# Block 3's state projection by Strassen's scheme between two output pairs, with seeded accumulators, in a fused state-space and gated layer

## Chip, cores and metric

One core of a Trainium2 chip runs the whole program. The metric is the device time of one execution in microseconds (us), and lower is better. The engines are TensorE (PE, matmuls), VectorE (DVE), ScalarE (ACT), GpSimd (POOL) and the DMA queues.

## The reference

```python
xn = layernorm(A_x)                                  # 2048 x 512, bf16
# A: diagonal complex state space, P = 512 states
Bu = einsum("bld,pd->blp", xn, B_bar)                # the state projection
h_t = Lam_bar * h_{t-1} + Bu_t                       # over 2048 steps
yA = 2 * real(einsum("blp,dp->bld", h, Cmat)) + xn * Dskip
# B: gated feed-forward, F = 1792
yB = (silu(xn @ w1) * (xn @ w3)) @ w2
out = A_x + yA + yB
```

The kernel works on four blocks of 512 rows. Each block needs its gates (14 tiles of 128 features), its state projection (4 state tiles, real and imaginary), a scan, and two output products of 256 rows each. These eight products are called "pairs" 0 to 7; pairs 0 and 1 belong to block 0, pairs 2 and 3 to block 1, and so on.

## The kernel before: what the argument touches

The output products already use Strassen's scheme in Winograd's form: seven block products in place of eight, with sums of blocks made by DVE (S1 to S4 of the left factor, called row sums here, and others of the right one). So does the up side (`w3`) of 12 of the last block's 14 gate tiles (the up scheme). The state projection is plain:

```python
def bu(b):                                  # state projection of block b
    for hf in range(NPT // 2):
        u = up.tile([P, 2, 2, TBLK], BF16, name="u")
        ...
                    for dt in range(NDT):   # 32 matmuls of 512 columns in all
                        nc.tensor.matmul(out=ps, lhsT=bt[:, ri, dt, ...], rhs=xnT_blk[b][:, dt, :], ...)
                    nc.scalar.activation(out=u[:, j, ri, :], in_=ps, func=ACT.Copy)
```

One output pair is seven products of 11 matmuls each (256 columns), seven for the gates and then four for the states. A seed is a value that is put into an accumulator in PSUM before the matmuls add to it. These are a pair's seeds, its fourth and its seventh product:

```python
def seeds(n):
    ...                                     # PSUM tiles g, e, f, z
    for t, cols in halves:                  # ACT puts the residual into e
        nc.scalar.activation(out=t, in_=o2[:, DH + cols.start:DH + cols.stop], func=ACT.Copy)

def product4():
    mms(z, v["a22"], tsum[3], True)
    ...
def product7():
    mms(g, v["s3"], tsum[2], False)
    add(q[2], g, o2[:, D1])                 # three adds on DVE
    add(o2[:, D2], g, q[1])
    add(o2[:, D1], z, q[2])
    store(c1 + 1, o2)
```

DVE's queue is put in order while the program is built. A small model, `Filler`, counts the microseconds given to PE (`bg.tensor`) and to DVE (`bg.own`, and a cost for each background task), and it lets background work in when DVE is not too far ahead:

```python
def own(self, us, after=0.1):
    self.dve = max(self.dve, self.pe + after) + us
def fill(self, lead=None):
    limit = self.pe + (self.lead if lead is None else lead)
    while self.tasks and self.dve + 0.5 * self.tasks[0][0] <= limit:
        ...
        self.pop()
```

The end of the program, in order, before the change:

```python
bu(3)
posts = ssm_tasks(3, True, between=up_sums(3))
...
y_fast(2, ...); y_fast(3, ...)
gate = glu_last(3)                          # the last block's gates ("gate stretch")
gate()
for n in range(4, 8): y_fast(n, ...)
```

## Time and profile before

The median is 203.09 us in three runs (202.9 to 203.15). The first table of the profile's page gives each engine's busy time, its share of the span and its instructions (PEld is the loading of weights, which overlaps PE):

```profile
span 201.1 us, 3551 instructions
## 1 busy us (share of the span) xinstructions
PE 197.2 (98%) x1353; PEld 126.4 (63%) x1353; DVE 180.4 (90%) x256; ACT 127.2 (63%) x257; POOL 47.9 (24%) x70
```

A busy PE can still contain gaps, because the recorded matmuls overlap: those of 512 columns are recorded as 379 ns long and start 216 ns apart. Start times are the better reading: from 8.2 us to the last matmul at 197.95 us, one matmul starts 216 ns (512 columns), 109 ns (256) or 56 ns (128) after the last. After the start there is one gap over 0.03 us. In the timeline of PE (start, duration, instruction, count, and in brackets the idle time before it and what ended it) it is the second line, where 0.67 us separate two starts of which 0.33 us are three matmuls of 256 columns:

```profile
85.80 0.49 PE L865 MATMUL gu_ps<-tw 128*128 128x256 f16 x3
86.47 0.82 PE L539 MATMUL gu_ps<-xnT,w_sb 128*128 128x512 bf16 x3 [0.18 <-DMA xnT<-xn]
```

The gap is 0.34 us long: block 2's gates wait for its transposed input, and only the 0.18 us in which the modelled matmuls don't cover it is listed as a wait.

The table of windows sums each engine's busy time in stretches that I cut at the first matmul of each stage. They are pairs 0 and 1; state projection of block 3 with pairs 2 and 3; gate stretch; pairs 4 to 7:

```profile
core 0: us, PE busy (x) PEld busy (x) DVE busy (x) ACT busy (x) POOL busy (x), PEclk, DMA share, GB/s
69.32:86.47 17.15, 16.97 (x155) 14.98 (x154) 16.56 (x25) 13.29 (x34) 4.66 (x7) 1.00 0.58 109
117.56:141.28 23.72, 23.72 (x188) 18.21 (x186) 21.78 (x30) 7.45 (x15) 6.56 (x5) 1.00 0.68 99
141.28:164.33 23.05, 23.05 (x151) 14.47 (x148) 22.09 (x32) 17.86 (x33) 0.86 (x1) 1.00 0.40 66
164.33:197.95 33.62, 33.62 (x330) 30.39 (x329) 26.36 (x44) 5.12 (x15) 2.84 (x2) 1.00 0.31 53
```

PE is the bound in all of them, with DVE close behind (21.78 of 23.72, 22.09 of 23.05). The tail, from the timeline of all engines (lines of PE left out), has three DVE adds of the seventh product, then two of the third:

```profile
196.98 0.42 DVE L876 TENSOR_TENSOR q<-y_ps,xn 128x256 f32<-128x256 f32 x1 [2.00 <-PE y_ps L865]
...
197.65 0.41 DVE L876 TENSOR_TENSOR xn<-y_ps,q 128x256 bf16<-128x256 f32 x1
...
198.09 0.81 SPq L882 DMA_DIRECT2D out_dram<-xn  x2
198.21 0.29 DVE L876 TENSOR_TENSOR xn<-gu_ps,x_blk 128x128 bf16<-128x128 f32 x1
198.53 0.37 ACTq L882 DMA_DIRECT2D out_dram<-xn  x1
```

### The profile page before, as it was taken

The numbers are of one execution on the slowest core, as the hardware profiler recorded it, in microseconds if no ns is written. First come the engines' busy times: TensorE is split into PE (matmuls) and PEld (weight loads), VectorE is DVE, ScalarE is ACT, GpSimd is POOL, SyncE is SP. The second block draws the span as 40 slices with busy tenths as digits, with TensorE's granted clock in tenths as the row PEclk, the third lists the DMA queues.
The fourth block names the chain that finished last, engine by engine and source line by source line (L and its number), as shares of the span: only waits on it lengthen the run. The fifth ranks groups of instructions, "written<-read, shape, count | busy, mean of one in ns | idle before, by whom it ended". The sixth has DMA issues, their size and how long they took to land.

```text
span 201.1 us, 3551 instructions
## 1 busy us (share of the span) xinstructions
PE 197.2 (98%) x1353; PEld 126.4 (63%) x1353; DVE 180.4 (90%) x256; ACT 127.2 (63%) x257; POOL 47.9 (24%) x70
## 2 busy tenths in 40 slices
PE   8999999999999999999999999999999999999994
PEld 2974444444444588844444445888566678888893
DVE  4699699999999999989999989998989998988833
ACT  4799788699999967957797676110588771101110
POOL 7160289600310053043005011315100003100000
PEclk9999999999999999999999999999999999999999
DMA  5999995980582043925895955294960002951011
GB/s 160 328 248 258 290 157 170 347 216 0 105 156 55 0 91 68 177 87 106 132 157 104 97 106 108 17 156 80 163 148 0 3 0 15 113 104 52 10 62 39
DMA packets 34225, 23.56 MB, mean 117 GB/s; under 512 B 21792, under 2 KB 32160, under 8 KB 34208
## 3 DMA queue, kind: packets, MB, share of 16 engines
q0 software_dynamic: 8096, 9.84, 32.3%
q1 hardware_dynamic: 25536, 13.21, 26.6%
q10 hardware_dynamic: 576, 0.30, 0.5%
q8 instruction: 10, 0.16, 0.3%
q14 instruction: 7, 0.06, 0.1%
HBM read 7.74 MB, written 2.10 MB: 49 GB/s over the span
## 4 chain that ended last, share of the span: by engine, by line
PE 59%; DVE 33%; DMA 3%; issue 2%; POOL 1%; ACT 1%; DVEq 0%
PE gu_ps L865 13%; PE gu_ps L539 12%; PE y_ps L865 7%; PE gu_ps L671 7%; PE bu_ps L865 4%; DVE u L484 4%; DVE act L557 4%; PE y_ps L438 3%; PE bu_ps L438 3%; PE y_ps L693 3%; DMA xnT<-xn 3%; DVE tw L796 2%; PE bu_ps L194 2%; DVE u L467 2%; DVE p L463 2%
## 5 line engine op out<-in xcount | busy, mean ns | idle before, releaser
L539 PE MATMUL gu_ps<-xnT,w_sb 128*128 128x512 bf16 x312 | 68.2, 379 | 0.2 <-DMA xnT<-xn 0.2
L539 PEld LDWEIGHTS <-w_sb 128*128 128x128 bf16 x312 | 30.4, 98 | 36.8 <-DMA xnT<-xn 0.5
L865 PEld LDWEIGHTS <-act 128*128 128x128 f16 x462 | 43.5, 98 | 5.4
L549 ACT ACTIVATE u<-gu_ps 128x512 bf16<-128x512 f32 x41 | 24.8, 606 | 5.8 <-PE gu_ps L539 5.1
L548 ACT ACTIVATE g<-gu_ps 128x512 bf16<-128x512 f32 x41 | 24.7, 603 | 5.4 <-PE gu_ps L539 5.1
L438 PEld LDWEIGHTS <-bt 128*128 128x128 bf16 x128 | 12.5, 98 | 15.1
L484 DVE TENSOR_TENSOR_SCAN u<-rho,act,u 128x512 bf16<-128x512 f32 x16 | 19.8, 1269 | 0.0
L824 POOL DMA_DIRECT2D act<-act x4 | 8.0, 2002 | 33.8 <-DVE tw L820 28.9
L865 PE MATMUL gu_ps<-w_sb,act 128*128 128x256 bf16 (+3 forms) x126 | 15.9, 267 | 0.0
L671 PE MATMUL gu_ps<-xnT,w_sb 128*128 128x512 bf16 x64 | 15.9, 379 | 0.0
L438 PE MATMUL y_ps<-xnT,bt 128*128 128x512 bf16 x64 | 15.1, 379 | 0.0
L438 PE MATMUL bu_ps<-xnT,bt 128*128 128x512 bf16 x64 | 15.1, 379 | 0.0
L557 DVE TENSOR_TENSOR act<-g,u 128x1024 f16<-128x1024 bf16 x21 | 14.2, 678 | 0.6 <-ACT u L549 0.6
L501 POOL DMA_DIRECT2D act<-p x7 | 6.3, 907 | 32.2 <-DVE act L494 28.2
L683 ACT ACTIVATE g<-gu_ps 128x512 bf16<-128x512 f32 x14 | 8.4, 598 | 5.7 <-PE gu_ps L671 5.3
L440 ACT ACTIVATE u<-y_ps 128x512 bf16<-128x512 f32 x16 | 9.5, 595 | 2.3 <-PE y_ps L438 2.1
L440 ACT ACTIVATE u<-bu_ps 128x512 bf16<-128x512 f32 x16 | 9.5, 595 | 2.0 <-PE bu_ps L438 1.9
L865 PE MATMUL bu_ps<-w_sb,act 128*128 128x256 bf16 (+3 forms) x84 | 10.4, 264 | 0.0
L865 PE MATMUL gu_ps<-ct,act 128*128 128x256 f16 (+1 forms) x72 | 10.4, 267 | 0.0
L484 DVE TENSOR_TENSOR_SCAN u<-rho,ends,u 128x512 bf16<-128x512 f32 x8 | 10.0, 1271 | 0.0
L467 DVE TENSOR_TENSOR u<-u,tabe 128x2048 bf16<-128x2048 bf16 x8 | 9.8, 1220 | 0.1
L490 DVE TENSOR_TENSOR p<-u,tabe 128x2048 f16<-128x2048 bf16 x8 | 9.8, 1220 | 0.1
(163 smaller groups left out, 342.3 us busy)
## 6 DMA issues: line engine op xcount, KB each, us to landing
act<-p POOLq DMA_DIRECT2D x7, 512.0 KB, 5.2
xn<-x_blk POOLq DMA_DIRECT2D x4, 512.0 KB, 5.8
out_dram<-xn SPq DMA_DIRECT2D x15, 128.0 KB, 2.6
w_sb<-in_B_w_dram SPq DMA_DIRECT2D x1, 1792.0 KB, 8.0
w_sb<-in_B_w_dram SPq DMA_DIRECT2D x2, 768.0 KB, 5.9
u<-x_blk POOLq DMA_DIRECT2D x3, 512.0 KB, 6.5
act<-act POOLq DMA_DIRECT2D x4, 352.0 KB, 6.8
w_sb<-in_B_w_dram SPq DMA_DIRECT2D x4, 256.0 KB, 4.3
```

Source lines behind the costliest of these rows:

```text
L438: nc.tensor.matmul(out=ps, lhsT=bt[:, ri, dt, pt * P:(pt + 1) * P], rhs=xnT_blk[b][:, dt, :], start=(dt == 0), stop=(dt == NDT - 1))
L440: nc.scalar.activation(out=u[:, j, ri, :], in_=ps, func=ACT.Copy)
L467: nc.vector.tensor_tensor(out=st["g"], in0=st["g"], in1=tabe[:, psl, 0:1, :].to_broadcast(FULL), op=ALU.mult)
L484: nc.vector.tensor_tensor_scan(out=v, data0=rho[:, pt:pt + 1].to_broadcast([P, TBLK]), data1=v, initial=init, op0=ALU.mult, op1=ALU.add)
L490: nc.vector.tensor_tensor(out=st["p16"][:, :, ::-1, :], in0=st["g"], in1=tabe[:, psl, 1:3, :], op=ALU.mult)
L539: nc.tensor.matmul(out=ps[:, tsl], lhsT=w[:, dt, f * P:(f + 1) * P], rhs=xnT[:, dt, tsl], start=(dt == 0), stop=(dt == NDT - 1))
L548: nc.scalar.activation(out=g16[:, f % 2, :], in_=g_ps, func=ACT.Silu)
L549: nc.scalar.activation(out=u16[:, f % 2, :], in_=u_ps, func=ACT.Copy)
L557: nc.vector.tensor_tensor(out=act(b)[:, k0:k1 + 1:k1 - k0, :], in0=g16, in1=u16, op=ALU.mult)
L671: nc.tensor.matmul(out=ps, lhsT=w[:, dt, f * P:(f + 1) * P], rhs=xnT[:, dt, :], start=(dt == 0), stop=(dt == NDT - 1))
L683: nc.scalar.activation(out=g16[:, f % 2, :], in_=side(w1_sb, f), func=ACT.Silu)
L865: nc.tensor.matmul(out=out, lhsT=left[:, k, :], rhs=right[k][:, cols], start=(start and k == 0), stop=(k == NK - 1), skip_group_check=True)
```

## The change

The intent is fewer columns on PE. The state projection of the last block is done by seven products in place of eight, one after another between the products of pairs 2 and 3. The sums of weights that this needs are written over the weights, which nobody needs afterwards. To make room on DVE, ACT seeds the accumulator Z (one DVE add less in each pair), S4 of pair 5 is an accumulating DMA, the up scheme covers 8 gate tiles rather than 12, and block 3's scans come later.

```diff
-    NG = 3
+    NG = 2
+    LATER = (4, 5)
+    def bu_fast(b, hf):            # returns five steps of seven products
+        def product(out, left, right, start=False):
+            for h in range(2):
+                for k in range(2):
+                    nc.tensor.matmul(out=out[:, h * TH:(h + 1) * TH], lhsT=left[:, h, k, :], rhs=right[:, k, :], ...)
+        def five():
+            product(e, s13, t1, True)
+            copy(s5, e)
+            subtract(s13, a22, s2)
 ...
+        return deque(((one, five), (two, six), (seven,), (three,), (four,)))
 ... in seeds():
+        nc.scalar.activation(out=z, in_=o2[:, D1], func=ACT.Copy)
 ... in y_fast():
-            mms(z, v["a22"], tsum[3], True)
+            mms(z, v["a22"], tsum[3], False)
+            copy(q[2], z)
-            add(q[2], g, o2[:, D1])
+            add(o2[:, D1], g, q[2])
             add(o2[:, D2], g, q[1])
-            add(o2[:, D1], z, q[2])
+            if n == 5:
+                gp.dma_start(out=v["s4"], in_=v["s2"], accum_op=ALU.add)
+            if i == 3 and n in LATER:
+                later[n] = product3        # done after product 5 of the next pair
 ... at the end:
-    bu(3)
-    posts = ssm_tasks(3, True, between=up_sums(3))
+    ssm_tasks(3, middle=[(0.0, after_y2, None), *row_sums(4, *pairs[4])])
-    y_fast(2, row_sums(3, *pairs[3]))
+    y_fast(2, row_sums(3, *pairs[3]), bu_fast(3, 0))
-    y_fast(3, row_sums(4, *pairs[4]))
+    y_fast(3, (), bu_fast(3, 1))
```

Left out are the sums' helpers, the homes of buffers, signs of some differences that were turned so that a DMA can add, and where in the program some tasks (seeds, gate multiplications, single row sums) are put in.

More of the change, by code (lines that the diff above doesn't have):

```diff
@@ L294, in ln_scalar_engine @@
             for cl in range(CPB):
-                spread.append((("ln", b, fn is norm and cl == CPB - 1), lambda fn=fn, cl=cl: fn(cl)))
+                spread.append(((fn.__name__, b, cl), lambda fn=fn, cl=cl: fn(cl)))
     NP3 = 3 * NPT
@@ L458, in pre_a @@
                 st["g"] = u_blk[b, hf]
-                if b == NBLK - 1 or (b, hf) == (2, 1):
-                    st["p"] = x_blk[2 if b == 2 else 2 + hf].rearrange("p (j r) t -> p j r t", r=2)
+                if (b, hf) in ((2, 1), (3, 0)):
+                    st["p"] = x_blk[b].rearrange("p (j r) t -> p j r t", r=2)
+                elif b == NBLK - 1:
+                    st["p"] = xtp.tile([P, NDT, TBLK], BF16, name="xnT").rearrange("p (j r) t -> p j r t", r=2)
                 else:
@@ L478, in scan @@
                 init = 0.0
-                if b == 1:
+                if b in (1, 2):
                     init = ends[:, hf, 2 * j + ri:2 * j + ri + 1]
-                elif b > 1:
+                elif b > 2:
                     init = act_blk[b - 1][:, k_state(pt, ri), TBLK - 1:TBLK]
@@ L501, in post_c @@
                     gp.dma_start(out=act_state(b, hf), in_=st["p16"], accum_op=ALU.add)
+            if (b, hf) == (1, 1):
+                pre_c.ready = lambda: ("squares", 2, CPB - 1) in sins_done
             pre_a.ready = lambda: (b, hf) in u_blk
@@ L640, with column_sums, run, column_list @@
     ups = {}
+    def column_sums(b):
+        def run():
+            for fn in column_list(b) + bu_first_sums():
+                fn()
+        run.ready = lambda: ("norm", b, CPB - 1) in sins_done
+        return [(2.1, run, "cols")]
+    def column_list(b):
+        xnT = xnT_blk[b]
+        t = x_blk[2].bitcast(FP16).rearrange("p a (k t) -> p a k t", k=2)
+        t1, t2, t3, t4 = (t[:, i] for i in range(4))
+        b11, b12, b21, b22 = (xnT[:, 2 * i:2 * i + 2, j * TH:(j + 1) * TH] for i in range(2) for j in range(2))
+        ups.update(t=(t1, t2, t3, t4), b=(b11, b12, b21, b22))
+        return [lambda out=out, x=x, z=z: nc.vector.tensor_tensor(out=out, in0=x, in1=z, op=ALU.subtract)
+                for out, x, z in ((t1, b12, b11), (t2, b22, t1), (t3, b22, b12), (t4, b21, t2))]
@@ new lines, in bu_quarter, with bu_first_sums, copy, parts @@
+    def bu_quarter(hf, kh, r, half=False):
+        v = bt[:, :, 2 * kh:2 * kh + 2, (2 * hf + r) * P:(2 * hf + r + 1) * P]
+        return v.bitcast(FP16) if half else v
+    def bu_first_sums():
+        return [lambda hf=hf: nc.vector.tensor_tensor(
+            out=bu_quarter(hf, 0, 1, True), in0=bu_quarter(hf, 0, 1), in1=bu_quarter(hf, 1, 1), op=ALU.add)
+            for hf in range(2)]
+    def bu_fast(b, hf):
+        t1, t2, t3, t4 = ups["t"]
+        b11, b12, b21, b22 = ups["b"]
+        a11, a12, a22 = bu_quarter(hf, 0, 0), bu_quarter(hf, 1, 0), bu_quarter(hf, 1, 1)
+        s2, s4, s13 = (bu_quarter(hf, *i, True) for i in ((0, 0), (1, 0), (0, 1)))
+        u = up.tile([P, 2, 2, TBLK], BF16, name="u")
+        s5 = glup.tile([P, 2, TBLK], BF16, name="g16").bitcast(FP32).rearrange("p a t -> p (a t)")
+        if hf == 0:
+            f, z = (ps_bu.tile([P, TBLK], FP32, name="bu_ps") for _ in range(2))
+            e, g = (ps_y.tile([P, TBLK], FP32, name="y_ps") for _ in range(2))
+        else:
+            f, z, e, g = (ps_gu.tile([P, TBLK], FP32, name="gu_ps") for _ in range(4))
+        def product(out, left, right, start=False):
+            for h in range(2):
+                for k in range(2):
+                    nc.tensor.matmul(out=out[:, h * TH:(h + 1) * TH], lhsT=left[:, h, k, :], rhs=right[:, k, :],
+                                     start=(start and h == 0 and k == 0), stop=(k == 1), skip_group_check=True)
+            bg.tensor(0.436)
+        def copy(out, x):
+            nc.scalar.activation(out=out, in_=x, func=ACT.Copy)
+        def parts(ps):
+            return ps.rearrange("p (h t) -> p h t", h=2)
+        def subtract(out, x, y):
+            bg.own(0.4)
+            nc.vector.tensor_tensor(out=out, in0=x, in1=y, op=ALU.subtract)
+        def add(out, ps):
+            bg.own(0.7)
+            nc.vector.tensor_tensor(out=out, in0=parts(ps), in1=parts(s5), op=ALU.add)
+        def one():
+            product(g, a11, b11, True)
+            copy(f, g)
+            subtract(s2, s13, a11)
+        def five():
+            product(e, s13, t1, True)
+            copy(s5, e)
+            subtract(s13, a22, s2)
+        def two():
+            product(f, a12, b21)
+            subtract(s4, a12, s2)
+            copy(u[:, 0, :, 0:TH], parts(f))
+        def six():
+            product(g, s2, t2)
+            copy(e, g)
+        def seven():
+            product(g, s13, t3)
+            copy(z, g)
+            add(u[:, 1, :, TH:TBLK], g)
+        def three():
+            product(e, s4, b22)
+            add(u[:, 0, :, TH:TBLK], e)
+        def four():
+            product(z, a22, t4)
+            copy(u[:, 1, :, 0:TH], parts(z))
+            u_blk[b, hf] = u
+        return deque(((one, five), (two, six), (seven,), (three,), (four,)))
@@ L642, in up_sums @@
     def up_sums(b):
-        xnT = xnT_blk[b]
         n = 4 * NG * P
@@ L649, in up_sums @@
         s3 = up_quarter(0, 1, True)
-        t = xtp.tile([P, NDT, TBLK], BF16, name="xnT").bitcast(FP16).rearrange("p a (k t) -> p a k t", k=2)
-        t1, t2, t3, t4 = (t[:, i] for i in range(4))
-        b11, b12, b21, b22 = (xnT[:, 2 * i:2 * i + 2, j * TH:(j + 1) * TH] for i in range(2) for j in range(2))
-        ups.update(s=(s1, s2, s3, up_quarter(1, 0, True)), t=(t1, t2, t3, t4), b=(b11, b12, b21, b22),
-                   s5=bt_flat[:, 0:2 * TBLK].bitcast(FP32))
-        return [(cost, lambda out=out, x=x, z=z, op=op: nc.vector.tensor_tensor(out=out, in0=x, in1=z, op=op), "up")
-                for cost, out, x, z, op in ((0.45, t1, b12, b11, ALU.subtract), (0.95, s1, a21, a22, ALU.add),
-                                    (0.45, t2, b22, t1, ALU.subtract), (0.95, s3, a11, a21, ALU.subtract),
-                                    (0.45, t3, b22, b12, ALU.subtract), (0.95, s2, s1, a11, ALU.subtract),
-                                    (0.45, t4, b21, t2, ALU.subtract))]
+        ups.update(s=(s1, s2, s3, up_quarter(1, 0, True)), s5=bt_flat[:, 0:2 * TBLK].bitcast(FP32))
+        return [(0.95, lambda out=out, x=x, z=z, op=op: nc.vector.tensor_tensor(out=out, in0=x, in1=z, op=op), "up")
+                for out, x, z, op in ((s1, a21, a22, ALU.add), (s3, a11, a21, ALU.subtract),
+                                      (s2, s1, a11, ALU.subtract))]
     def glu_last(b):
@@ L703, in add @@
             nc.vector.tensor_tensor(out=out, in0=halves(ps), in1=halves(s5), op=ALU.add)
-        first = pair_tiles()
+        gates = []
         for f in range(4 * NG, NFT):
-            gate_side(f, first[0])
-            copy(first[1][:, f % 2, :], side(w3_sb, f))
+            if f % 2 == 0:
+                tiles = pair_tiles()
+            gate_side(f, tiles[0])
+            copy(tiles[1][:, f % 2, :], side(w3_sb, f))
             bg.fill()
-        gates = [lambda: gate(NFT - 2, first)]
+            if f % 2 == 0 and gates:
+                gates.pop()()
+            if f % 2 == 1:
+                gates.append(lambda f=f, tiles=tiles: gate(f - 1, tiles))
         for n in range(NG):
@@ L794, in add @@
         def add(i, which):
-            out, x, z = ((t1, b12, b11), (t2, b22, t1), (t3, b22, b12), (t4, b21, t2))[which]
+            out, x, z = ((t1, b12, b11), (t2, t1, b22), (t3, b22, b12), (t4, b21, t2))[which]
             bg.add((1.1, 0.7)[i], lambda: nc.vector.tensor_tensor(
-                out=out[i], in0=x[i], in1=z[i], op=ALU.subtract), "tw")
+                out=out[i], in0=x[i], in1=z[i], op=ALU.add if which == 3 else ALU.subtract), "tw")
         return add
@@ L820, in subtract @@
             return lambda: nc.vector.tensor_tensor(out=out, in0=x, in1=z, op=ALU.subtract)
-        return [(0.9, subtract(s3, a11, a21), ("sums", n)),
-                (0.9, lambda: nc.vector.tensor_tensor(out=a21, in0=a21, in1=a22, op=ALU.add), ("sums", n)) if n in (0, 1, 6, 7) else
-                (0.0, lambda: gp.dma_start(out=a21, in_=a22, accum_op=ALU.add), ("sums", n)),
-                (0.9, subtract(s2, a22, s3), ("sums", n))]
+        three = (0.9, subtract(s3, a11, a21), ("sums", n))
+        two = (0.9, subtract(s2, s3, a22), ("sums", n))
+        if n in (0, 1, 6, 7):
+            one = (0.9, lambda: nc.vector.tensor_tensor(out=a21, in0=a21, in1=a22, op=ALU.add), ("sums", n))
+        else:
+            one = (0.0, lambda: gp.dma_start(out=a21, in_=a22, accum_op=ALU.add), ("sums", n))
+        return [three, two, one] if n > 5 else [three, one, two]
     seeded = {}
@@ L847, in seeds, with y_fast @@
         seeded[n] = g, halves, f, z
-    def y_fast(n, then=()):
+    later = {}
+    def y_fast(n, then=(), between=()):
         b, p = pairs[n]
@@ L853, in y_fast @@
         bg.flush("tw")
-        if p == 0 and b > 0:
+        if p == 0 and b > 1:
             bg.flush(("scan", b + 1))
@@ L859, in y_fast @@
         g, halves, f, z = seeded[n]
+        q0 = x_blk[2].rearrange("p c d -> p (c d)")[:, 0:2 * DH].bitcast(FP32) if n == 5 else q[0]
         tsum = [weight(0, D2, True)] + [[tw[:, i, k, :] for k in range(NK)] for i in range(3)]
@@ L902, in product2 @@
             v["s4"] = v["a12"]
-            bg.own(0.85, -1.1)
-            nc.vector.tensor_tensor(out=v["s4"], in0=v["a12"], in1=v["s2"], op=ALU.subtract)
+            if n == 5:
+                gp.dma_start(out=v["s4"], in_=v["s2"], accum_op=ALU.add)
+            else:
+                bg.own(0.85, -1.1)
+                nc.vector.tensor_tensor(out=v["s4"], in0=v["a12"], in1=v["s2"], op=ALU.add)
             add(o1[:, D1], f, o1[:, D1])
@@ L907, in product2 @@
                 store(c1, o1, D1)
-            if n + 1 < len(pairs) and n not in (1, 3):
+            if n + 1 < len(pairs) and n not in (1, 2, 3) and n - 1 not in LATER:
                 seeds(n + 1)
@@ L914, in product3 @@
                 mms(t, v["s4"], weight(1, D2), False, cols)
-                add(o1[:, right(cols)], t, q[0][:, cols])
+                add(o1[:, right(cols)], t, q0[:, cols])
                 if last:
@@ L924, in product4 @@
         def product4():
-            mms(z, v["a22"], tsum[3], True)
+            mms(z, v["a22"], tsum[3], False)
+            copy(q[2], z)
             steps()
-            bg.fill(1.2 if b > 0 else None)
+            bg.fill(1.2 if b > 0 and n not in LATER else None)
         def product5():
@@ L938, in product6 @@
             mms(g, v["s2"], tsum[1], False)
-            add(q[0], g, o1[:, D2].bitcast(FP16))
+            add(q0, g, o1[:, D2].bitcast(FP16))
             steps()
@@ L954, in y_fast @@
         for i in ((1, 5, 2, 6, 4, 3, 7) if b == 0 else (1, 4, 2, 6, 5, 7, 3)):
-            products[i - 1]()
+            if i == 3 and n in LATER:
+                later[n] = product3
+            else:
+                products[i - 1]()
+            if i == 5 and n - 1 in later:
+                later.pop(n - 1)()
+                if n + 1 < len(pairs):
+                    seeds(n + 1)
+            if n in LATER:
+                bg.fill()
+            if between:
+                for step in between.popleft():
+                    step()
+                    bg.fill()
+                if n == 3 and not between:
+                    bg.first(up_sums(3))
+            if n == 2 and i == 7:
+                seeds(3)
     ln_alloc(0)
@@ L990, with after_y2, keep_ends @@
         weight_sum(i, which)
-    kept = []
-    def keep_ends():
-        if kept:
+    y_done = []
+    def after_y2():
+        pass
+    after_y2.ready = lambda: 2 in y_done
+    kept = set()
+    def keep_ends(b):
+        if b in kept:
             return
-        kept.append(True)
-        nc.vector.tensor_copy(out=ends, in_=act(0).rearrange("p (h k) t -> p h k t", h=2)[:, :, NFH:NK, TBLK - 1])
-    ssm_tasks(1, between=[(0.2, keep_ends)])
+        kept.add(b)
+        nc.vector.tensor_copy(out=ends, in_=act(b).rearrange("p (h k) t -> p h k t", h=2)[:, :, NFH:NK, TBLK - 1])
+    ssm_tasks(1, between=[(0.2, lambda: keep_ends(0))])
     gate = glu(1)
@@ L1003 @@
     bg.flush(("sums", 0))
-    bg.first([(0.0 if kept else 0.2, keep_ends, ("ends", 0))])
-    bg.flush(("ends", 0))
+    keep_ends(0)
     y_fast(0, row_sums(1, *pairs[1]))
@@ L1008 @@
     y_fast(1)
-    sin_step(("ln", 2, True))
+    sin_step(("norm", 2, CPB - 1))
     for cl, o in held:
@@ L1012 @@
     res_difference(1)
-    ssm_tasks(2, between=row_sums(2, *pairs[2]), late=res_list(3))
+    ssm_tasks(2, between=[(0.2, lambda: keep_ends(1)), *row_sums(2, *pairs[2])], late=res_list(3) + column_sums(3))
     gate = glu(2)
     gate()
-    sin_step(("ln", 3, True))
+    sin_step(("norm", 3, CPB - 1))
     res_difference(2)
     seeds(2)
-    bu(3)
-    posts = ssm_tasks(3, True, between=up_sums(3))
+    bg.flush("cols")
+    ssm_tasks(3, middle=[(0.0, after_y2, None), *row_sums(4, *pairs[4])])
     res_difference(3)
-    posts()
-    y_fast(2, row_sums(3, *pairs[3]))
-    bg.flush(("ssm", 2))
-    y_fast(3, row_sums(4, *pairs[4]))
+    keep_ends(1)
+    y_fast(2, row_sums(3, *pairs[3]), bu_fast(3, 0))
+    y_done.append(2)
+    y_fast(3, (), bu_fast(3, 1))
     bg.flush("up")
```

## The prediction

> **What bounds the kernel now.** The first table of the profile has TensorE (PE) busy 197.2 of 201.1 us, VectorE (DVE) 180.4, ScalarE (ACT) 127.2. Busy matmuls can hide gaps, so I read the timeline by start times: from 8.2 us to the last matmul at 197.95 us one matmul starts 216 ns after the last (512 columns) or 109 ns (256), almost everywhere. The Trainium skill ("TensorE: Matmul & The Clock Gate", section "Back-to-back issue gap") gives N/2.4 + 2.5 ns, which is 215.8 and 109.2: the trace agrees. The only real gap after the start is 0.34 us at 86.5 us (a transposing DMA; the waits view names 0.2 us of it). The matmul stream is the bound, so a change gains only by removing columns or by shortening the tail (3.2 us after the last matmul starts). DVE is second: 97% busy from 90 to 165 us (table of windows), though nearly never waited for.
>
> **What the change does, costed.**
> - State projection of block 3: 32 matmuls of 512 columns (6.91 us on PE) become 56 of 256 (6.10 us): -0.81 us.
> - Up scheme on 8 tiles in place of 12: 4 plain products of 0.864 us replace 7 of 0.436 us: +0.41 us.
> - ACT's seeds of Z, S4 by DMA, the delayed third product: no columns change.
>
> Net on PE: -0.40 us, all of it critical.
>
> DVE: eight output adds at 0.33 us go (-2.7), S4 of pair 5 (-0.8), smaller and fewer up sums (about -2.6, estimated from 0.95, 0.42 and 0.65 us operations); ten sums on the state weights (+3.4 at 0.34), four adds from PSUM (+2.6), one copy. DVE's total hardly moves (-0.1 to -1 us). ACT gains about 3 us of copies and seeds and loses PSUM evacuations, and has room. DVE's gain is off the critical path.
>
> What moves: the projection's 6 us used to give DVE time before pair 2; now its products are spread between those of pairs 2 and 3, the scans of block 3 come later (half 1 in pair 4, its closing products in pair 5), and DVE has less lead before pair 6. Walking both queues with the trace's durations (an estimate), pairs 2 and 3 meet their deadlines with 0.3 to 2 us to spare. Two places are tight: (a) the last gate stretch, where the row sum of pair 4 waits for the accumulating DMA of block 2's second half (5.2 us to landing), after which the adds that free the y banks come within about 0.3 us of the next products; (b) the fourth product of pair 6, which now needs ACT's seed of Z, itself after DVE's residual difference, late by perhaps 0.3 us. I expect 0.2 us of stalls together. The tail's last two adds wait for PE anyway, so one add fewer there gives at most 0.1 us.
>
> **Prediction.** 203.09 - 0.40 + 0.2 = 202.9 us, range 202.4 to 203.7. Faster by over 2%: 0.01; within 2%: 0.97; slower: 0.02.
>
> **Right or wrong.** Right: matmul count up by 12, spacing still 216/109 ns, pair 4 starts about 0.4 us earlier than 164.5 us, DVE busy within 2 us of before, no new PE wait over 0.5 us. Wrong, step by step: a PE wait inside pairs 2 or 3 on DVE's weight sums or ACT's copies (the interleaving fails); PE waits in the last gate stretch (a) or at pair 6 (b) over 0.5 us; a wait on the S4 DMA, for which I count 4 us of slack.
>
> **What would make it wrong.** In-order DVE stuck behind one late DMA, so that every later sum is late: that could cost 1 to 2 us. Or no stall at all and a shorter tail: 202.5.

## The result, and the profile after

The changed kernel took 202.34 us (median of four, 201.91 to 202.79) against 203.12 for the kernel before in the same session. The ratio is 0.9963 (0.9938 to 0.9987). Ratios here are the mean time of one kernel's fast runs over that of the other's in the same rounds, so they are not quite the ratios of the medians. Repeated later on another occasion the medians were 202.18 and 203.26 us, ratio 0.9957 (0.9939 to 0.9975). The gain is about 0.4%, clear of noise but far below 2%; the time lies just under the predicted range.

```profile
span 200.4 us, 3599 instructions
## 1 busy us (share of the span) xinstructions
PE 195.2 (97%) x1353; PEld 127.0 (63%) x1365; DVE 179.9 (90%) x257; ACT 133.4 (67%) x275; POOL 50.1 (25%) x71
```

Weight loads rose by the 12 expected. The 1353 matmul records did not, since twelve of this trace are missing; their places are gaps of exactly one matmul, most of them 10.8 us apart, and I leave them out below. The second trace of this kernel (after_again) has all 1365 and none of these gaps. The waits of PE (engine and tile, what it waited for, total us, times, longest) name nothing after the first 10 us:

```profile
PE bu_ps L195 <- PEq L1179: 0.8, 1, 0.8
PE y_ps L242 <- DVE xn L223: 0.6, 1, 0.6
PE gu_ps L576 <- DMA w_sb<-in_B_w_dram: 0.4, 1, 0.4
```

The gap before block 2 is gone; the first matmul of its gates starts right behind the pair:

```profile
86.38 0.81 PE L544 MATMUL gu_ps<-xnT,w_sb 128*128 128x512 bf16 x2
```

The same windows as before:

```profile
core 0: us, PE busy (x) PEld busy (x) DVE busy (x) ACT busy (x) POOL busy (x), PEclk, DMA share, GB/s
69.57:86.38 16.81, 16.81 (x156) 15.00 (x154) 16.26 (x23) 13.97 (x38) 4.64 (x6) 1.00 0.56 109
117.46:140.38 22.92, 22.92 (x211) 20.55 (x210) 21.41 (x36) 10.73 (x23) 2.84 (x2) 1.00 0.50 75
140.38:163.82 23.44, 23.28 (x136) 13.31 (x137) 22.24 (x29) 17.28 (x31) 4.56 (x4) 1.00 0.60 94
163.82:197.44 33.62, 33.62 (x330) 30.35 (x329) 27.14 (x42) 7.73 (x23) 4.79 (x3) 1.00 0.45 64
```

The stretches, from start times of matmuls; "tail" runs from the last matmul's start to the end:

| stretch | before | after | difference |
|---|---|---|---|
| start, to the first 512-column gate matmul | 12.34 | 12.59 | +0.25 |
| blocks 0 and 1 | 56.98 | 56.98 | 0 |
| pairs 0 and 1 | 17.15 | 16.81 | -0.34 |
| block 2 | 31.09 | 31.08 | -0.01 |
| state projection of block 3, pairs 2 and 3 | 23.72 | 22.92 | -0.80 |
| gate stretch | 23.05 | 23.43 | +0.38 |
| pairs 4 to 7 | 33.62 | 33.62 | 0 |
| tail | 3.19 | 2.97 | -0.22 |
| span | 201.15 | 200.41 | -0.74 |

The start differs between any two traces, of one kernel too: 12.34 and 12.62 us in two traces of the kernel before, 12.59 and 12.54 in two of the changed one, 12.20 to 12.97 over all that I took. It is the noise of these times. The other stretches came back within 0.05 us. Apart from the start the change is worth 0.99 us in these traces: 0.42 us of columns, 0.34 us of the gap at 86.5 us, and 0.22 us of tail. Only the first stood in the predicted sum.

In the tail, two DVE adds of the seventh product are left, and the SP queue's two stores (one of full width, then one of 128 columns) begin to go out 0.70 us ahead of the ACT queue's last one (128 columns), not 0.44:

```profile
196.54 0.42 DVE L981 TENSOR_TENSOR xn<-y_ps,q 128x256 bf16<-128x256 f32 x1 [2.07 <-PE y_ps L970]
...
197.32 0.81 SPq L987 DMA_DIRECT2D out_dram<-xn  x2
197.70 0.29 DVE L981 TENSOR_TENSOR xn<-gu_ps,x_blk 128x128 bf16<-128x128 f32 x1 [0.20 <-PE gu_ps L970]
198.02 0.35 ACTq L987 DMA_DIRECT2D out_dram<-xn  x1
```

### The profile page after: what moved, and what is told of

The parts are those of the page before. It is cut to its first block, busy times and chain, and to the rows that moved or that the text cites. A ratio compares the mean times of both kernels' runs of the same rounds, so it can differ in the third digit from the quotient of the medians.

```text
span 200.4 us, 3599 instructions
## 1 busy us (share of the span) xinstructions
PE 195.2 (97%) x1353; PEld 127.0 (63%) x1365; DVE 179.9 (90%) x257; ACT 133.4 (67%) x275; POOL 50.1 (25%) x71
## 4 chain that ended last, share of the span: by engine, by line
PE 95%; DMA 2%; SPq 1%; issue 0%; DVE 0%
PE gu_ps L544 33%; PE gu_ps L970 17%; PE y_ps L970 10%; PE gu_ps L764 9%; PE bu_ps L970 7%; PE y_ps L439 5%; PE bu_ps L439 5%; PE y_ps L786 2%; DMA w_sb<-in_B_w_dram 2%; PE gu_ps L576 2%; PE gu_ps L689 2%; PE y_ps L689 1%; PE bu_ps L576 1%; PE bu_ps L786 1%; PE bu_ps L689 0%
## 5 line engine op out<-in xcount | busy, mean ns | idle before, releaser
L544 PE MATMUL gu_ps<-xnT,w_sb 128*128 128x512 bf16 x306 | 67.8, 379 | 0.3
L544 PEld LDWEIGHTS <-w_sb 128*128 128x128 bf16 x312 | 30.4, 98 | 36.4
L487 DVE TENSOR_TENSOR_SCAN u<-rho,ends,u 128x512 bf16<-128x512 f32 x16 | 19.9, 1272 | 0.0
L764 PE MATMUL gu_ps<-xnT,w_sb 128*128 128x512 bf16 x77 | 18.4, 379 | 0.2
L439 PEld LDWEIGHTS <-bt 128*128 128x128 bf16 x96 | 9.4, 98 | 11.3
L764 PEld LDWEIGHTS <-w_sb 128*128 128x128 bf16 x80 | 7.8, 98 | 7.5
L439 PE MATMUL y_ps<-xnT,bt 128*128 128x512 bf16 x47 | 11.3, 379 | 0.1
L439 PE MATMUL bu_ps<-xnT,bt 128*128 128x512 bf16 x46 | 11.2, 379 | 0.1
L487 DVE TENSOR_TENSOR_SCAN u<-rho,act,u 128x512 bf16<-128x512 f32 x8 | 9.9, 1270 | 0.0
L497 DVE TENSOR_TENSOR act<-u,tabe 128x2048 f16<-128x2048 bf16 x8 | 9.7, 1218 | 0.0
```

The costliest lines, as they stand in the source:

```text
L439: nc.tensor.matmul(out=ps, lhsT=bt[:, ri, dt, pt * P:(pt + 1) * P], rhs=xnT_blk[b][:, dt, :], start=(dt == 0), stop=(dt == NDT - 1))
L487: nc.vector.tensor_tensor_scan(out=v, data0=rho[:, pt:pt + 1].to_broadcast([P, TBLK]), data1=v, initial=init, op0=ALU.mult, op1=ALU.add)
L497: nc.vector.tensor_tensor(out=act_state(b, hf), in0=st["g"], in1=tabe[:, psl, 0:1, :].to_broadcast(FULL), op=ALU.mult)
L544: nc.tensor.matmul(out=ps[:, tsl], lhsT=w[:, dt, f * P:(f + 1) * P], rhs=xnT[:, dt, tsl], start=(dt == 0), stop=(dt == NDT - 1))
L764: nc.tensor.matmul(out=ps, lhsT=w[:, dt, f * P:(f + 1) * P], rhs=xnT[:, dt, :], start=(dt == 0), stop=(dt == NDT - 1))
```

## The experiments

Theory A: PE's stream is the only thing that counts, and the unpredicted 0.56 us is chance. Theory B: the seeds of Z shorten the tail, close the gap before block 2, and give DVE the lead without which the new schedule stalls. Eleven runs were made (nine edited kernels and a repeat of each of the two), each in five rounds, all with correct results.

| run | median us | ratio to before (95%) |
|---|---|---|
| before_again | 202.91 | 0.9988 (0.9971 to 1.0005) |
| z_alone | 202.90 | 0.9983 (0.9966 to 1.0000) |
| after_no_z | 206.32 | 1.0153 (1.0134 to 1.0172) |
| after_again | 202.18 | 0.9957 (0.9939 to 0.9975) |
| no_z_same_order2 | 203.61 | 1.0017 (0.9995 to 1.0039) |
| z_not_last2 | 202.49 | 0.9973 (0.9952 to 0.9994) |
| after_ng3_2 | 204.50 | 1.0067 (1.0049 to 1.0086) |
| after_s4_dve2 | 203.23 | 1.0004 (0.9983 to 1.0025) |
| z_not_first | 202.65 | 0.9986 (0.9955 to 1.0017) |
| s4_both_dma | 203.48 | 1.0027 (0.9999 to 1.0056) |
| ng3_s4_both | 204.77 | 1.0089 (1.0066 to 1.0112) |

The rows fall into three sessions of four, four and three kernels; the medians of before were 203.26, 202.97 and 202.90 us. Times scatter by 0.5 us and more because of the start, so for tenths of a microsecond I read the stretches of the traces, which don't.

### before_again and after_again: what repeats

No edit. Expected:

> The unchanged kernel, as a null test and for a second trace. Ratio 1.000 within 0.002. If the 0.34 us gap of PE at 86.5 us (the transposing DMA of block 2) and the 2.62 us from the last store's issue to the end belong to this kernel, both are there again within 0.1 us; if they were chance of one execution, they move by 0.2 us or more. The start (up to the first full-width gate matmul, 12.34 us in one trace, 12.59 in that of the changed kernel) moves by some 0.2 us either way, since the programs do not differ there.

> The changed kernel, for a second trace and for its time on the same chip as the two parts. 202.3 us, ratio 0.9963 within 0.0015. No gap of PE over 0.1 us between 13 us and the last matmul; PE from the first product of pair 2 to the start of the gate stretch 22.9 us, gate stretch 23.4 us, pairs 4 to 7 33.6 us, each within 0.05 us.

Measured: the gap before block 2 is again there in the kernel before (0.29 us) and absent in the changed one, the tails are 3.19 and 2.97 us again, the start moved (12.62 and 12.54 us). The stretches of the changed kernel came back as 22.92, 23.43 and 33.62 us. So gap and tail belong to the kernels and are not chance.

### z_alone: the seeds of Z on the kernel before

```diff
+        nc.scalar.activation(out=z, in_=o2[:, D1], func=ACT.Copy)
-            mms(z, v["a22"], tsum[3], True)
+            mms(z, v["a22"], tsum[3], False)
+            copy(q[2], z)
-            add(q[2], g, o2[:, D1])
+            add(o2[:, D1], g, q[2])
             add(o2[:, D2], g, q[1])
-            add(o2[:, D1], z, q[2])
```

> The kernel before with ACT's seeds of Z alone; no column of PE changes. Theory (PE columns alone explain the gain, the rest is chance): ratio 1.000, no change over 0.1 us. Rival (the seeds also shorten the tail, since the store before the last leaves one add earlier, and free DVE and ACT in pairs 0 and 1 so that the transposes of block 2 land in time): -0.2 to -0.6 us, ratio 0.997 to 0.999, with the last full-width store issued about 0.3 us earlier against the last matmul.

Measured: tail 2.98 us; gap before block 2 0.12 us, pairs 0 and 1 16.93 us (from 17.10 to 17.15). A new gap of 0.25 us in pair 3 takes over half of it back: DVE's changed order puts a row sum, which waits 1.28 us for an accumulating DMA, ahead of that product's work. The time alone doesn't decide (ratio 0.9983, interval up to 1.0000); the stretches do, and they speak for B.

### after_no_z: the changed kernel without the seeds of Z

The edit is the reverse of the one above, on the changed kernel.

> The changed kernel with the seeds of Z undone: eight more adds of 0.33 us on DVE. Theory (columns alone): 202.3 us, no change against the changed kernel. Rival: the tail gives back 0.2 us, the transposes up to 0.34 us, and pair 6, whose fourth product had 0.5 us to spare, stalls 0.1 to 0.3 us because pairs 4 and 5 carry two more adds: 202.6 to 203.0 us.

Measured: 206.32 us. Neither theory had this size: the 0.4% gain becomes a 1.5% loss. PE has a gap of 1.74 us in pair 2 and of 0.34 and 1.41 us in pair 6. The first, from the timelines of PE and of DVE:

```profile
118.64 0.60 PE L689 MATMUL y_ps<-xnT,bt 128*128 128x256 bf16 x4
120.82 0.61 PE L689 MATMUL y_ps<-x_blk,bt 128*128 128x256 f16 x4 [1.58 <-DVE bt L669]
```

```profile
115.34 1.29 DVE L562 TENSOR_TENSOR act<-g,u 128x1024 f16<-128x1024 bf16 x2
118.27 0.69 DVE L562 TENSOR_TENSOR act<-g,u 128x1024 f16<-128x1024 bf16 x1 [1.64 <-ACT u L554]
118.88 0.42 DVE L661 TENSOR_TENSOR x_blk<-xnT 128x512 f16<-128x512 bf16 x1
...
120.34 0.75 DVE L669 TENSOR_TENSOR bt<-bt 128x512 f16<-128x512 bf16 x2
```

The last gate multiplication (118.27) waits 1.64 us for ACT, and the sums on which the projection's products wait stand behind it. In the changed kernel they stand ahead of it and are done at 119.02 us, 0.08 us before the product that needs them starts. The program's own model of DVE, told of 0.35 us more per add, had moved them. So two things changed: DVE's work, and its order.

### no_z_same_order2: work without order

```diff
-            add(q[2], g, o2[:, D1])
+            nc.vector.tensor_tensor(out=q[2], in0=g, in1=o2[:, D1], op=ALU.add)   # not told to the model
```

> The changed kernel without the seeds of Z, as before (206.3 us), but the extra add is not told to the model by which the program orders DVE's queue, so the queue keeps the changed kernel's order with eight adds put in. Theory A (the 4 us came of the new order: the sums for the state products put behind the last gate): 202.9 to 203.5 us, no gap of PE over 0.4 us at pair 2. Theory B (the 0.33 us per pair themselves break the deadlines of pairs 2 and 6): 205.5 us or more, the gaps of 1.7 and 1.4 us stay. In both the tail is 3.2 us and the gap before block 2 is 0.3 us again.

Measured: 203.61 us, 0.1 above the range of the first. The trace has DVE's instructions in the changed kernel's order, but for the adds themselves. Pairs 2 and 3 take 22.93 us without a gap; pairs 4 to 7 34.19 us (+0.57, a gap at pair 6's sixth product, which waits for a row sum); the gap before block 2 is 0.46 us and the tail 3.28 us. Pair 6's gap:

```profile
184.37 1.38 PE L969 MATMUL gu_ps<-tw,x_blk 128*128 128x256 f16 x11 [0.40 <-DVE x_blk L918]
```

Against the changed kernel's stretches that is 0.01 + 0.57 + 0.46 + 0.31 = 1.35 us for the eight adds (with ACT's eight seeds and eight copies gone). The rest of after_no_z's loss is the order. Of the 4 us, then, about a third comes with the order kept, and two thirds are the queue's order.

### z_not_last2: the tail

```diff
+        if n < 7:
             nc.scalar.activation(out=z, ...)      # and the three adds again in the last pair
```

> The changed kernel with the seed of Z undone in the last pair alone; the stream up to the last matmul is the same. Theory (the seed shortens the tail because the next to last store leaves one add earlier and is out of the way of the last one): tail 3.2 us in place of 2.97, that store issued 0.3 us later against the last matmul, time +0.2 us. Rival (the tail differs by chance): tail 2.97 us.

Measured: every stretch as in the changed kernel, tail 3.20 us. The DVE work and the last store, from the timeline:

```profile
197.65 0.81 SPq L988 DMA_DIRECT2D out_dram<-xn  x2
197.76 0.29 DVE L982 TENSOR_TENSOR xn<-gu_ps,x_blk 128x128 bf16<-128x128 f32 x1
198.09 0.37 ACTq L988 DMA_DIRECT2D out_dram<-xn  x1
```

The last add ends at the same distance from the last matmul (0.55 us after its start in both traces), so it was not delayed. The last store landed 1.70 us after issue here and in the kernel before, against 1.48 us in both traces of the changed kernel. In the slower ones the SP queue's second store and the last one go out within 0.01 us of each other; with one add fewer they are 0.27 us apart. The traces' DMA packets (in the packed trace; no view lists them by time) show more. Counted from the last matmul's start, the packets of the full-width store, of the SP queue's small one and of the last one run to 1.52, from 1.46 to 1.76 and from 1.58 to 1.87 us here; in the changed kernel to 1.24, from 1.20 to 1.48 and from 1.44 to 1.71 us. The three move nearly one behind the other, and the add saved lets the first of them leave earlier. What they share inside, the runs don't show.

### z_not_first: the gap before block 2

The same with `n > 1`: no seeds in pairs 0 and 1 alone, the model not told.

> The changed kernel with the seeds of Z undone in pairs 0 and 1 alone, DVE's order otherwise kept. Theory (the gap before block 2 closes because of the seeds there): pairs 0 and 1 take 17.1 to 17.2 us in place of 16.81, the gap of 0.3 us before block 2 is back, the rest of the stream is unchanged within 0.1 us, tail 2.97 us; time +0.3 us, 202.5 us. Rival (something else of the change closes it): pairs 0 and 1 stay at 16.8 to 16.9 us.

Measured: pairs 0 and 1 17.15 us, gap 0.34 us, all else as in the changed kernel, DVE's order too:

```profile
87.11 1.25 PE L544 MATMUL gu_ps<-xnT,w_sb 128*128 128x512 bf16 x5 [0.17 <-DMA xnT<-xn]
```

So the seeds in pairs 0 and 1 close the gap. The edit swaps one DVE add in each pair for a seed and a copy on ACT, so it can't tell DVE's part from ACT's, and how the seeds do it stays open. The transposes were issued at the same time (10.48 and 11.79 us after pair 0's start for the last two, against 10.50 and 11.81 in the changed kernel), and so was the accumulating DMA that runs beside them; but the last of them landed at 17.11 rather than 16.73 us. It is the transfers that took longer, not their issue. The packets give a lead that no run tests: a packet of 8192 bytes on queue 14, which the profile calls instruction, begins 15.56 to 15.72 us after pair 0's start in the five traces without these seeds, and at 12.87 to 13.51 us in the eight with them. Between 15 and 17 us, 13 to 22 packets of the transposes' and stores' queue take over 0.4 us in the five, 7 in z_alone and none in the other seven. In all thirteen ACT has 177 to 180 instructions on record when that packet begins, and the seeds and copies bring ACT there earlier. So the gap may come of when ACT's instructions are fetched, and not of DVE's adds. In z_alone, with the same seeds, 0.12 us of gap remained; there the last transpose was issued only at 13.00 us.

### after_s4_dve2: how much room pair 6 has

```diff
-            if n == 5:
+            if n == -1:                            # S4 of pair 5 on DVE again
                 gp.dma_start(out=v["s4"], in_=v["s2"], accum_op=ALU.add)
```

> The changed kernel with S4 of pair 5 on DVE again (0.8 us) in place of the accumulating DMA. Theory (pair 6 has 0.5 us to spare): PE gaps of 0.3 to 0.6 us at the fourth and sixth product of pair 6, 202.6 to 202.9 us. Rival (DVE has spare time there): no gap, 202.2 us.

Measured: 203.23 us, one gap of 1.0 us at pair 6's sixth product, which waits for the row sum `x_blk`:

```profile
184.02 1.38 PE L970 MATMUL gu_ps<-tw,x_blk 128*128 128x256 f16 x11 [0.83 <-DVE x_blk L918]
```

The direction was right, the size not: I had counted 0.5 us of room, and it was nearly none. Here the model moved the order a little too (a multiplication of the scan went behind an add), so that the row sum ended 1.05 us later, not S4's 0.8 us. In the changed kernel this is how close it runs (DVE's lines, then PE's fourth and sixth product):

```profile
178.97 1.22 DVE L502 TENSOR_TENSOR act<-act,p 128x2048 f16<-128x2048 f16 x1
...
182.02 0.89 DVE L918 TENSOR_TENSOR x_blk<-x_blk,act 128x1408 f16<-128x1408 f16 x1
```

```profile
180.63 1.36 PE L970 MATMUL gu_ps<-tw,act 128*128 128x256 f16 x11
...
183.03 1.36 PE L970 MATMUL gu_ps<-tw,x_blk 128*128 128x256 f16 x11
```

The sixth product needs what DVE finished at 182.91 (0.12 us to spare). The fourth needs what it finished at 180.19, but for its last four matmuls alone, 0.76 us after its start: 1.2 us to spare. The 0.5 us that I had counted was read at its start.

### after_ng3_2: all 12 tiles by the up scheme

`NG = 3` in the changed kernel, which is 0.41 us fewer columns.

> The changed kernel with the up scheme on all 12 gate tiles as before the change: 0.41 us fewer columns on PE, some 2.6 us more on DVE in the gate stretch. Theory A (PE's columns alone count): gate stretch 23.05 us, 201.8 us in all. Theory B (DVE has no room left: its last work before pair 6 ended 0.5 us before the product that needs it): gate stretch 23.05 us or a little more, but a gap of 1 to 2.5 us in pairs 4 to 6, 203 to 204.5 us in all.

Measured: 204.50 us, at the upper end of what B gave. The gate stretch did fall to 23.05 us; pairs 4 to 7 rose from 33.62 to 36.05. PE in pair 6, where the fourth product's first seven matmuls ran in time and the last four waited:

```profile
182.46 0.61 PE L970 MATMUL gu_ps<-tw,act 128*128 128x256 f16 x4 [1.16 <-DVE act L502]
...
185.19 1.38 PE L970 MATMUL gu_ps<-tw,x_blk 128*128 128x256 f16 x11 [0.91 <-DVE x_blk L918]
```

These are the two deadlines named above. This is why the change gives up 0.38 us of columns again. The model moved DVE's order here as well, so work and order are not told apart.

### s4_both_dma and ng3_s4_both: relief by another DMA

```diff
-            if n == 5:
+            if n in (4, 5):
                 gp.dma_start(out=v["s4"], in_=v["s2"], accum_op=ALU.add)
```

and the same with `NG = 3`.

> The changed kernel with S4 of pair 4 by DMA too: 0.8 us less on DVE just where 0.8 us more (pair 5 on DVE) cost 1.0 us. Theory (PE's stream has no gap left, so relief buys nothing by itself): 202.2 us, no change over 0.1 us in any stretch. Rival (DVE's time is worth time everywhere): -0.3 to -0.8 us.

> The up scheme on 12 tiles with S4 of pair 4 by DMA too; the 12-tile version alone took 204.5 us, with 2.4 us of gaps in pair 6. Theory (those gaps are DVE's lateness, so 0.8 us of relief ahead of them closes 0.6 to 0.9 us of them): pairs 4 to 7 35.1 to 35.5 us in place of 36.05, 203.5 to 203.9 us in all; still behind the changed kernel. Rival (the gaps come of the order or of a transfer): 36 us or more.

Measured: 203.48 and 204.77 us; pairs 4 to 7 take 34.69 and 36.19 us. In s4_both_dma both theories failed, since the relief made things worse. In ng3_s4_both the rival's range held (36 us or more). PE's waits in the first, from its timeline:

```profile
177.36 0.94 PE L970 MATMUL gu_ps<-w_sb,act 128*128 128x256 bf16 x7 [0.32 <-DMA act<-x_blk]
...
181.10 0.61 PE L970 MATMUL gu_ps<-ct,act 128*128 128x256 f16 x4 [0.40 <-DMA act<-p]
```

DVE was in time there (its last state sum ended at 178.95 us, 1.1 us earlier after pair 4's start than in the changed kernel), but PE waited for transfers. DVE's order had changed too; the waits that the trace names are for DMAs. In s4_both_dma the accumulating DMAs issued at 166.29, 167.96, 169.33 and 174.94 us landed at 173.89, 177.31, 181.06 and 184.49: 3.4 to 3.8 us apart however early they were issued, and up to 11.7 us after issue. In the changed kernel, with one fewer, they took 6.6, 6.3 and 6.7 us. The Trainium skill ("DMA: Bandwidth & Descriptors", section "SWDGE vs HWDGE vs iDMA") says that accumulation in a DMA is open to GpSimd's path alone and that only one such queue is allocated; landings one after another agree with that. In ng3_s4_both PE waits 1.4 us for the same transfer, of S4 of pair 4. So the DMA way out was used up too.

No version beat the changed kernel.

## Why the prediction was wrong, point by point

The columns were right. Three terms of the sum were not: 0.2 us of stalls that did not come, 0.22 us of tail and the 0.34 us of a gap taken as fixed. They make 0.76 us in the two traces, of which the start, as noise, took 0.25 us back. Behind the last two is one step, "DVE's gain is off the critical path": the seeds of Z, which give this gain, brought both (z_not_first, z_not_last2). The prediction did name "no stall at all and a shorter tail: 202.5" as a way to be wrong; the gap it did not.

- **PE's columns: right.** "Net on PE: -0.40 us, all of it critical." Measured -0.80 and +0.38 us, together -0.42. The spacing of 216 and 109 ns is what the Trainium skill ("TensorE: Matmul & The Clock Gate", section "Back-to-back issue gap") gives with N/2.4 + 2.5 ns, there for an isolated matmul, before and after.
- **"I expect 0.2 us of stalls together": wrong, there were none.** Place (a), the row sum of pair 4, did wait for its DMA (0.8 us in DVE's waits), but PE did not feel it. Place (b) was misread. The seed of Z reads the second row group of the pair, and the residual difference writes the first, so they don't depend on each other; ACT put the seed down from 177.51 to 177.89 us, 2.7 us before the product that needs it.
- **"One add fewer there gives at most 0.1 us": wrong, 0.22 us.** It was right that the last adds wait for PE. The step left out the stores: with one add fewer the full-width store leaves earlier, and the last lands sooner (z_not_last2).
- **The gap at 86.5 us: missed.** I had named it and left it as it was. The seeds in pairs 0 and 1 close it (z_not_first), 0.34 us.
- **"DVE's gain is off the critical path": the step that failed in kind.** The seeds that give it brought 0.34 us before block 2 and 0.22 us of tail (if ACT's part and not DVE's closes the gap, the step failed for another reason there). The rest of it is off the path only as long as it is there. Take it away, and 1.35 us come back with the order kept, and 4 us when the order follows (no_z_same_order2, after_no_z). The same goes for the 0.8 us of S4 (after_s4_dve2, 1.0 us with its change of order). I had counted "0.3 to 2 us to spare"; the trace shows 0.08 us at pair 2 and 0.12 us at pair 6.
- **"a wait on the S4 DMA, for which I count 4 us of slack": no wait, but little to add.** One more such transfer was enough to make PE wait (s4_both_dma).
- **Sizes on other engines.** DVE's busy time fell by 0.5 us, inside the -0.1 to -1 predicted. ACT's rose by 6.2 us where I had said about 3 and some off; it had the room.

The sum as it should have stood: -0.42 columns, no stalls, -0.34 transposes, -0.22 tail, which is -0.98 us; the two sessions showed -0.78 and -1.08 us between medians.

What stays open is by what path the seeds in pairs 0 and 1 shorten the transposes' transfer (the instruction packet is a lead, not shown), and what the last three stores share.

## What to carry to other kernels

When one engine's stream has no gaps, look at what each of the others must finish by, and by how much it makes it: a busy share of 90% can mean 0.1 us of room, and relief that shows no gain of its own may be what lets the other half of a change work. Judge such relief by taking it away, with the queue's order held fixed, since a schedule built from a cost model can turn a third of a microsecond into four. And ask of each small item saved what follows it, to the last store, and whether the place it moves to (here an accumulating DMA) still has room.

## What the Trainium skill lacked or had wrong

- "DMA: Bandwidth & Descriptors", section "Anatomy of one DMA — SWDGE (gpsimd) path", fits 2.0 us + bytes / 436e3. For 352 KB (360,448 bytes) that gives an estimate of 2.8 us. An accumulating transfer of this size inside SBUF took 6.6 to 7.0 us from issue to landing in the changed kernel, and with others ahead of it up to 10.3 us (ng3_s4_both); one of 512 KB took 4.5 us at the least, and 6.3 us (the changed kernel) and 11.7 us (s4_both_dma) with others ahead. The page has no figure for accumulation, nor one for several in a row (3.1 to 3.8 us from landing to landing in the last two runs).
- "TensorE: Matmul & The Clock Gate", section "Back-to-back issue gap", states for a stream of weight loads and matmuls about 131 ns for each matmul of 512 columns and about 81 ns for one of 128. This kernel loads weights for every matmul and ran at 216 ns and 56 ns; the formula that the section calls isolated is the one that held.
- No page has a figure for what a DMA transpose loses to other transfers of the same moment: the last one of block 2 landed 16.73 us after pair 0's start in the changed kernel and 17.11 us in z_not_first, issued at the same time; of what, stays open.
- No page has a figure for small stores close behind one another on two queues: the last one of 32 KB landed 1.70 us after issue when the one before it went out within 0.01 us, and 1.48 us when they were 0.27 us apart.
